# Queries loaded without zeros, and matrix products of ones ahead of the first loads

## The chip, the core and the metric

The kernel runs on one core of a Trainium2 chip. Five engines work side by side, each with its own queue of instructions: TensorE (PE; its weight loads are listed apart as PEld), VectorE (DVE), ScalarE (ACT), GpSimd (POOL) and SyncE (SP), which here issues every DMA. The metric is the device time of one execution in microseconds (us), the median of several runs; lower is better.

## The reference

Attention over 8 batches, 8 heads, 576 positions and 64 features per head, followed by a mixing block:

```python
scores = scale * np.matmul(q, k.transpose(0, 1, 3, 2))
mask_plain = (rel >= 0) & (rel < 32)                              # heads 0..3
mask_dil = (rel >= 0) & (rel < 128) & (rel % 4 == 0)              # heads 4..7
attn = softmax(np.where(masks, scores, -1e9))
x = np.matmul(attn, v)            # heads side by side: (8, 576, 512)
theta = x @ w_theta
y = w_tok_r @ (x * cos(theta)) + w_tok_i @ (x * sin(theta))
u = x + y
out = u + np.maximum(u @ w_ch, 0.0)
```

Each query sees 32 keys at most. Positions of the dilated heads are reordered on the host, so that their 32 keys lie side by side too.

## The kernel before

**Tiles of the attention.** Heads go in pairs (four pairs `pr` per batch `b`, 32 pairs in all). A pair has 18 blocks of 32 queries, and each block meets the 64 keys around it. `scores(b, pr)` (L441) makes one matmul per block (L468): the stationary operand is 128 x 64, 64 features of each of the two heads by 32 queries of each. It is block-diagonal: the half of a column that belongs to the other head is zero, so one matmul over 128 partitions serves both heads. The host array `qT` holds these zeros (L1006 to L1010), and so one pair's queries are 128 x 1152 words, of which half are zeros; they come with one DMA (L221, and L282 for batch 0). The keys come as 128 x 608 words (L223, L284). Matmuls of float32 appear twice in the trace, so the 18 blocks of a pair are 36 weight loads and 36 matmuls.

**Batch 0** goes ahead of all else. `first_loads` (L270) issues on SP, in this order: the masks, two identities, and queries and keys of the four pairs, then the values. The mask is added by matmuls of `mskb` with the identity `idb` (L424), and the score matmuls add onto it. DVE takes the row maximum and subtracts it (L430, L433), ACT exponentiates (L493), DVE sums (L495), POOL normalises (L510), PE transposes (L561, `flip`), and `pv` (L603) multiplies by the values (L617). ACT copies the result out of PSUM (L581, `x_evac`); for the pairs 2 and 3 that copy writes with a step of four words, since it undoes the reordering of positions. Then follow theta (L667), sines and cosines, the token mixing `y` (L850) and the channel mixing `c` (L882). Weights are unpacked on the way (`unpack`, L311; L332 is its first step on DVE).

**Order of the work.** Up to the middle of batch 1, the class `Order` sets the order: a planner that gives each task a rank and each step a cost, and starts on each engine the ready task with the lowest rank. Loads enter it by their words (`dma(2 * S)` for a pair's queries). What it lays out is pinned in that order on PE, DVE, ACT, POOL and SP. From then on `phase` (L889) writes the scores of the next batches, the mixing units and the values' products out in turn; PE keeps this order.

**Loads in flight.** A DMA signals one of eight semaphores, used in turn. A DMA therefore waits until the one issued eight before it has landed. In the steady part two buffers `q` (pool `attn`, L218) take turns, and the load of a pair waits for the scores two pairs back.

Of the kernel before, what the change touches and what calls it, by code (L numbers as in the profile page):

```python
# [8 lines left out]
F32 = mybir.dt.float32  # L9
# [28 lines left out]

FG0 = {4: ("zl2", "zl6"), 0: ("zl3", "zl7"), 1: ("zh3", "zh7")}
COS_PSUM, SIN_PSUM = True, True  # L40
KORD = (0, 4, 1, 5, 2, 6, 3, 7, 8)
TP0 = {4: "s", 0: "s", 1: "x", 2: "t", 3: "s"}
TP = {4: "t", 0: "s", 1: "s", 2: "t", 3: "s"}
# [108 lines left out]
def build(ctx, tc, qT, kT, vw, wth, wtk, wch, maskb, ident, identb, outT):  # L152
# [60 lines left out]
    def load_qk(n):  # L213
        if n >= B * NP:
            return
        b, pr = divmod(n, NP)
        r = yield from take("qk", 2)
        q = ap.tile([128, 2 * NJ, 2 * QB], F32, tag="q", name=f"q{b}_{pr}")  # L218
        k = ap.tile([128, S + 32], F32, tag="k", name=f"k{b}_{pr}")
        yield "DMA", dma(2 * S)  # L220
        pin(nc.sync.dma_start(q, qT[b, pr]))  # L221
        yield "DMA", dma(S + 32)
        pin(nc.sync.dma_start(k, kT[b, pr]))  # L223
        qks[b, pr] = (q, k, r)
        signal(("qk", b, pr))
# [12 lines left out]
    def load_vb(n):  # L238
# [12 lines left out]
        vs["b", b, pr] = (vb, r)  # L251
        signal(("vb", b, pr))

    KE = S + 32
    first_k = hp.tile([128, 10 * HS], F32R, tag="wt_b", name="first_k").bitcast(F32)
    first_v = hp.tile([128, 8 * HS], F32R, tag="wt_a", name="first_v").bitcast(F32)
# [13 lines left out]
    def first_loads():  # L270
# [3 lines left out]
        for pr in range(NP):  # L274
            yield from take(f"xh{pr}", 1, 0)
            yield from take(f"u{pr}", 1, 0)
            pqs.append(hp.tile([128, 2, S], F32R, tag=f"xh{pr}", name=f"P0_{pr}").bitcast(F32)[:, 0])
            q = hp.tile([128, 2, S], F32R, tag=f"u{pr}", name=f"q0_{pr}").bitcast(F32)
            q = q.rearrange("p a b -> p (a b)").rearrange("p (a b) -> p a b", b=2 * QB)
            k = first_k[:, KE * pr:KE * pr + KE]  # L280
            yield "DMA", dma(2 * S)
            pin(nc.sync.dma_start(q, qT[0, pr]))  # L282
            yield "DMA", dma(KE)
            pin(nc.sync.dma_start(k, kT[0, pr]))  # L284
            qks[0, pr] = (q, k, None)
            if pr == 0:
                yield "DMA", dma(128)
                pin(nc.sync.dma_start(idt, ident))
            signal(("qk", 0, pr))
# [11 lines left out]
    def consts():  # L301
        yield "DVE", 60
        pin(nc.vector.memset(halfpi, math.pi / 2))
        for n in range(2):
# [2 lines left out]
            pin(nc.gpsimd.memset(t, 0.0))  # L307
            pts.append(t)
        signal("pts")

    def unpack(src, sz, name, stage, early, n, key):  # L311

# [128 lines left out]
    def scores(b, pr):  # L441
# [3 lines left out]
        if pr >= 1:  # L445
            yield None, ("sc", b, pr - 1)
        q, k, rqk = qks[b, pr]
        if b == 0:
            P, rp = pqs[pr].rearrange("p (a b) -> p a b", b=BW), None
        else:  # L450
            rp = yield from take("P", 2)
            P = sp.tile([128, NJ, BW], F32, tag="P", name=f"P{b}_{pr}")
# [3 lines left out]
        for g0, g1 in ((0, 5), (5, NJ)):  # L456
# [8 lines left out]
            for n in range(g0, g1):  # L465
                for e in range(2):
                    qb = 2 * n + e
                    pe(nc.tensor.matmul(ps[64 * e:64 * e + 64, n - g0], q[:, qb],  # L468
                                        k[:, QB * qb:QB * qb + BW], start=not masked, stop=not masked or n == g1 - 1))
            if masked:  # L470
                go(row_max(b, ps, rel, P, mx, g0, g1, ("mask", b, pr, g0)))
# [481 lines left out]
    EA, LA, LA2 = ([(t, reserve(t)) for t in ts] for ts in (EARLY, LATE, LATE2))  # L953
    XH = {p: reserve(f"xh{p}") for p in range(NP)}
    UH = {d: reserve(f"u{d}") for d in range(NC)}
    od.live = True
    go(first_loads(), 0)
    go(consts(), 0)
# [36 lines left out]
def _arrays(inp):  # L995
# [7 lines left out]
        return a  # L1003

    q, k, v = perm(q), perm(k), perm(v)
    qT = np.zeros((B, NP, 2, D, 2 * NJ, 2, QB), q.dtype)  # L1006
    qh = q.reshape(B, NP, 2, 2 * NJ, QB, D).transpose(0, 1, 2, 5, 3, 4)
    for hh in range(2):
        qT[:, :, hh, :, :, hh] = qh[:, :, hh]
    qT = qT.reshape(B, NP, 128, 2 * NJ, 2 * QB)  # L1010
    kT = np.zeros((B, NP, 128, S + 32), k.dtype)
    kT[..., 32:] = k.transpose(0, 1, 3, 2).reshape(B, NP, 128, S)
    vp = np.zeros((B, H, S + 32, D), v.dtype)
# [45 lines left out]
```

## Time and profile before

| | |
|---|---|
| median of 3 runs | 577.83 us (577.48 to 578.81) |
| the profiled execution | 577.82 us |
| its span, first to last instruction | 576.0 us |
| PE, PEld busy | 550.5 us (96%), 501.6 us (87%) |
| DVE, ACT, POOL busy | 378.0, 345.2, 222.2 us |
| moved by DMA | 81.9 MB |

A row of the timeline gives start, duration, engine, line, operation, destination and sources, and how many instructions are merged into it; in brackets stands how long the engine had been idle before and what ended this. A row of the windows view gives the busy time of each engine in a stretch (with the number of instructions), then the TensorE clock that the throttle granted (1.00 is full), the mean busy share of the 16 DMA engines, and GB/s. In a row of the waits view stand the total, the number of waits and the longest. In the chain of waits each row is a start, a duration and what it was; "issue" is time without a recorded cause. DMA rows give the size of one and the median time from issue to landing.

### The profile page before, as it was taken

To read this page: it belongs to the slowest core of one execution; us is meant where nothing else is said; L and a number is where in the kernel's file an instruction comes from. 1 tells how busy PE (TensorE), PEld (TensorE's weight loads), DVE (VectorE), ACT (ScalarE), POOL (GpSimd) and SP (SyncE) were. 2 spreads that over 40 slices of the span, in tenths; PEclk is the share of its full clock that TensorE was granted. 3 is DMA by queue.
4 is the path that set the end of the run, shared out by engine and by line. 5 is a ranking of instruction groups with operands and counts; after the bars stand their busy time and mean duration, and the time that the engine had idled before them with its cause. 6 is when DMAs were issued, how large, how long until landed. Compare 5 with 4: busy or idle time off the path is not lost.

```text
span 576.0 us, 13996 instructions
## 1 busy us (share of the span) xinstructions
PE 550.5 (96%) x5464; PEld 501.6 (87%) x5464; DVE 378.0 (66%) x1156; ACT 345.2 (60%) x939; POOL 222.2 (39%) x206
## 2 busy tenths in 40 slices
PE   5997799999999999999999999999999999999997
PEld 4744688879999899988999899988999899989997
DVE  3879798865666668756776768756775767445112
ACT  1498967768555784369555785359556695266110
POOL 2228855525224352226324253226323353325220
PEclk9999699899999999999999999999999999999999
DMA  8991437601747046540746146550747123321002
GB/s 303 400 368 28 165 105 245 216 0 63 231 150 193 32 162 210 169 127 20 268 143 172 64 148 202 181 136 11 252 146 190 69 83 102 77 89 65 18 1 83
DMA packets 45586, 81.91 MB, mean 142 GB/s; under 512 B 3920, under 2 KB 19024, under 8 KB 45520
## 3 DMA queue, kind: packets, MB, share of 16 engines
q1 hardware_dynamic: 45520, 81.02, 43.7%
q8 instruction: 43, 0.70, 0.5%
q14 instruction: 23, 0.19, 0.1%
HBM read 64.49 MB, written 16.52 MB: 141 GB/s over the span
## 4 chain that ended last, share of the span: by engine, by line
DVE 34%; ACT 30%; PE 25%; issue 5%; POOL 2%; DMA 2%; SPq 0%; ACTq 0%; POOLq 0%; DVEq 0%
DVE pt L525 16%; PE y L850 11%; ACT P L504 11%; PE c L882 6%; PE th L685 3%; DVE P L409 3%; ACT K L698 3%; ACT K L787 3%; DVE xh L599 3%; ACT th L796 2%; ACT zh L644 2%; DVE xq L729 2%; DVE K L789 2%; ACT cos L705 2%; ACT x L581 2%
## 5 line engine op out<-in xcount | busy, mean ns | idle before, releaser
L830 POOL TENSOR_TENSOR u<-x,u 128x288 fp32r<-128x288 f32 x64 | 54.7, 858 | 184.6 <-ACT u L828 184.6
L525 DVE STREAM_TRANSPOSE pt<-P 32x288 f32<-32x288 f32 x224 | 105.1, 469 | 12.0 <-POOL P L510 8.9
L882 PE MATMUL c<-u,late_wc 128*128 128x288 f32 x768 | 110.2, 296 | 2.8 <-DVE x L859 2.8
L882 PEld LDWEIGHTS c<-u,late_wc 128*128 128x128 f32 x768 | 106.0, 188 | 6.8 <-DVE x L859 4.0
L850 PE MATMUL y<-wtkh,zh 128*128 128x288 f32 x288 | 90.3, 314 | 1.1 <-ACT zh L644 1.1
L850 PE MATMUL y<-wtkh,zl 128*128 128x288 f32 x288 | 86.2, 299 | 4.0 <-POOL zl L646 4.0
L646 POOL TENSOR_TENSOR zl<-g,zh 128x512 fp32r<-128x512 f32 x40 | 52.3, 1316 | 97.5 <-ACT zh L644 84.5
L504 ACT ACTIVATE P<-P,mx 128x64 f32<-128x64 f32 x216 | 72.0, 335 | 25.8 <-DVE mx L498 25.8
L850 PE MATMUL y<-wtkl,zh 128*128 128x288 f32 x288 | 85.9, 298 | 0.0
L828 ACT CAST u<-x 128x288 fp32r<-128x288 f32 x64 | 26.9, 429 | 86.2 <-DVE x L825 85.5
L685 PE MATMUL th<-wthh,xh 128*128 128x512 f32 x224 | 74.8, 395 | 0.3 <-DVE g L784 0.3
L850 PE MATMUL y<-late_wt_b,zh 128*128 128x288 f32 x320 | 68.1, 297 | 0.0
L825 DVE TENSOR_TENSOR x<-y,x 128x288 f32<-128x288 f32 x64 | 28.1, 448 | 53.6 <-PE y L850 53.5
L850 PEld LDWEIGHTS y<-wtkh,zl 128*128 128x128 f32 x288 | 55.1, 191 | 4.7 <-POOL zl L646 4.7
L850 PEld LDWEIGHTS y<-wtkh,zh 128*128 128x128 f32 x288 | 54.9, 191 | 4.7 <-ACT zh L644 2.3
L850 PE MATMUL y<-late_wt_a,zh 128*128 128x288 f32 x256 | 56.3, 301 | 0.0
L850 PEld LDWEIGHTS y<-wtkl,zh 128*128 128x128 f32 x288 | 55.1, 191 | 0.3 <-issue 0.3
L510 POOL TENSOR_TENSOR P<-P,sm 128x576 f32<-128x576 f32 x32 | 37.5, 1172 | 41.1 <-DVE sm L508 18.1
L850 PEld LDWEIGHTS y<-late_wt_b,zh 128*128 128x128 f32 x320 | 51.4, 189 | 0.3
L685 PEld LDWEIGHTS th<-wthh,xh 128*128 128x128 f32 x224 | 42.0, 188 | 9.2 <-DVE g L784 0.6
L850 PE MATMUL y<-late_wt_b,zl 128*128 128x288 f32 x160 | 47.4, 296 | 0.0
L581 ACT COPY x<-o 128x576 f32<-128x576 f32 x32 | 29.4, 919 | 28.4 <-PE o L617 19.1
(108 smaller groups left out, 1106.3 us busy)
## 6 DMA issues: line engine op xcount, KB each, us to landing
q<-in_qT_dram SPq DMA_DIRECT2D x32, 576.0 KB, 5.2
va<-in_vw_dram SPq DMA_DIRECT2D x30, 320.0 KB, 3.2
k<-in_kT_dram SPq DMA_DIRECT2D x28, 304.0 KB, 5.5
out_dram<-x SPq DMA_DIRECT2D x28, 288.0 KB, 2.4
vb<-in_vw_dram SPq DMA_DIRECT2D x29, 256.0 KB, 3.8
xd<-xq SPq DMA_DIRECT2D x24, 288.0 KB, 5.1
xn<-xd SPq DMA_DIRECT2D x24, 256.0 KB, 3.4
st_wtk<-in_wtk_dram SPq DMA_DIRECT2D x8, 576.0 KB, 8.8
```

The lines of the kernel that those rows point to most:

```text
L409: pin(nc.vector.tensor_tensor_reduce(out=P[:, n], in0=ps[:, n - g0], in1=mskb[:, mask_of(pr, n)], op0=ALU.add, op1=ALU.max, scale=1.0, sca ...
L504: table(nc.scalar.activation(P[:, n], P[:, n], AF.Exp, bias=mx[:, n:n + 1], scale=SCALE, accum_out=sm[:, n:n + 1]))
L510: pin(nc.gpsimd.tensor_tensor(P, P, sm.unsqueeze(2).to_broadcast([128, NJ, BW]), op=ALU.mult))
L525: pin(nc.vector.transpose(pmats[b, pr][k0:k0 + QB, :, hh, QB * e:QB * e + QB], P[p0:p0 + QB, :, QB * o:QB * o + QB]))
L581: pin(nc.scalar.copy(dst, src))
L646: pin(nc.gpsimd.tensor_tensor(lo, z, hi.bitcast(F32), op=ALU.subtract))
L685: pe(nc.tensor.matmul(pt, l, r, start=(n == 0), stop=(n == 3 * NC - 1)))
L825: pin(nc.vector.tensor_tensor(x[:, ts], ps, x[:, ts], op=ALU.add))
L828: pin(nc.scalar.copy(uh[b, d][:, ts], x[:, ts]))
L830: pin(nc.gpsimd.tensor_tensor(ul[b, d][:, ts], x[:, ts], uh[b, d][:, ts].bitcast(F32), op=ALU.subtract))
L850: pe(nc.tensor.matmul(ps, l[:, cs], r, start=(n == 0), stop=(n == 3 * NK - 1)))
L882: pe(nc.tensor.matmul(ps, l[:, cs], r[:, ts], start=(n == 0), stop=(n == 3 * NC - 1)))
```

## The change

Four things change.

- The host no longer writes the zeros. `qT` is 128 x 576 words per pair: 64 features of head one, then 64 of head two, and along a row the 18 blocks innermost (a query of position 32 n + r in its head lies at word 18 r + n).
- A pair's queries come with two DMAs of 64 x 576 words, each into its own half of the partitions and of the columns of a tile 128 x 2 x 576. The other halves are zeroed: in batch 0 by DVE, two memsets per pair; later two tiles `qbufs` take turns for the whole run and are zeroed once, by POOL.
- The stationary operand of a score matmul now is `q[:, :, qb]`: 64 columns with a step of 18 words (72 bytes), where it was 64 words side by side.
- DVE writes ones into a 128 x 512 bf16 tile ahead of all else, and PE multiplies it by itself 14 times into an unused PSUM tile ahead of its first mask matmul.

```diff
+WARM_UP = 14
...
-        q = ap.tile([128, 2 * NJ, 2 * QB], F32, tag="q", name=f"q{b}_{pr}")
+        q = qbufs[r % 2]
...
-        yield "DMA", dma(2 * S)
-        pin(nc.sync.dma_start(q, qT[b, pr]))
+        yield "DMA", dma(S)
+        for hh in range(2):
+            rs = slice(64 * hh, 64 * hh + 64)
+            pin(nc.sync.dma_start(q[rs, hh], qT[b, pr, rs]))
...
+    qbufs = [cp.tile([128, 2, S], F32, name=f"q{n}") for n in range(2)]
...
             q = hp.tile([128, 2, S], F32R, tag=f"u{pr}", name=f"q0_{pr}").bitcast(F32)
-            q = q.rearrange("p a b -> p (a b)").rearrange("p (a b) -> p a b", b=2 * QB)
+            for hh in range(2):
+                pin(nc.vector.memset(q[64 * hh:64 * hh + 64, 1 - hh], 0.0))
...
-            yield "DMA", dma(2 * S)
-            pin(nc.sync.dma_start(q, qT[0, pr]))
+            yield "DMA", dma(S)
+            for hh in range(2):
+                rs = slice(64 * hh, 64 * hh + 64)
+                pin(nc.sync.dma_start(q[rs, hh], qT[0, pr, rs]))
...
+        for q in qbufs:
+            for hh in range(2):
+                yield "POOL", 580
+                pin(nc.gpsimd.memset(q[64 * hh:64 * hh + 64, 1 - hh], 0.0))
...
+        q = q.rearrange("p h (r n) -> p (h r) n", n=2 * NJ)
...
-                    pe(nc.tensor.matmul(ps[64 * e:64 * e + 64, n - g0], q[:, qb],
+                    pe(nc.tensor.matmul(ps[64 * e:64 * e + 64, n - g0], q[:, :, qb],
...
+    ones = cp.tile([128, DM], BF16, name="ones")
+    nc.vector.memset(ones, 1.0)
+    busy = ps_v.tile([128, 2 * DM], F32, tag="v", name="busy")
+    for n in range(WARM_UP):
+        pe(nc.tensor.matmul(busy[:, :DM], ones[:, :128], ones, start=True, stop=True))
...
-    qT = np.zeros((B, NP, 2, D, 2 * NJ, 2, QB), q.dtype)
-    qh = q.reshape(B, NP, 2, 2 * NJ, QB, D).transpose(0, 1, 2, 5, 3, 4)
-    for hh in range(2):
-        qT[:, :, hh, :, :, hh] = qh[:, :, hh]
-    qT = qT.reshape(B, NP, 128, 2 * NJ, 2 * QB)
+    qT = q.reshape(B, H, 2 * NJ, QB, D).transpose(0, 1, 4, 3, 2).reshape(B, NP, 128, S)
```

The planner sees half the words for a query load and lays its part out anew. Three places matter.

SP at the start, before: the loads of batch 0 (`q_0` is pair 0's queries; all keys go into one tile `first_k`; DMAHWn is one of the eight semaphores of the loads).

```order
L282 DMA q_0_105<-in_qT_dram 128x1152
L284 DMA first_k<-in_kT_dram 128x608
L288 DMA idt<-in_ident_dram 128x128
L282 DMA q_1_115<-in_qT_dram 128x1152
L282 DMA q_2_122<-in_qT_dram 128x1152
L284 DMA first_k<-in_kT_dram 128x608 [waits DMAHW0_49]
L282 DMA q_3_155<-in_qT_dram 128x1152 [waits DMAHW1_49]
L284 DMA first_k<-in_kT_dram 128x608 [waits DMAHW2_49]
L293 DMA first_v<-in_vw_dram 128x1152 [waits DMAHW3_49]
```

SP at the start, now:

```order
L293 DMA q_0_123<-in_qT_dram 64x576 x2
L295 DMA first_k<-in_kT_dram 128x608
L299 DMA idt<-in_ident_dram 128x128
L293 DMA q_1_136<-in_qT_dram 64x576 x2
L295 DMA first_k<-in_kT_dram 128x608 [waits DMAHW0_49]
L293 DMA q_2_147<-in_qT_dram 64x576 [waits DMAHW1_49]
L293 DMA q_2_147<-in_qT_dram 64x576 [waits DMAHW2_49]
L295 DMA first_k<-in_kT_dram 128x608 [waits DMAHW3_49]
L293 DMA q_3_170<-in_qT_dram 64x576 [waits DMAHW4_49]
```

The order is the same, with two loads where there was one; so the wait for the load eight before comes after fewer pairs: with the keys of pair 1, where it was with those of pair 2.

PE at the start, before (`s_0_0` is the first half of pair 0's scores in PSUM):

```order
L424 LDWEIGHTS idb
L424 MATMUL s_0_0_118<-mskb,idb 128x64
L424 MATMUL s_0_0_118<-mskb,idb 128x256
L468 MATMUL s_0_0_118<-first_k,q_0_105 64x64 x10
L424 MATMUL s_0_5_135<-mskb,idb 128x256
```

PE at the start, now (the first two rows stand 14 times):

```order
L977 LDWEIGHTS ones
L977 MATMUL busy<-ones 128x512
L439 LDWEIGHTS idb [waits DMAHW1_49]
L439 MATMUL s_0_0_141<-mskb,idb 128x64 [waits DMAHW0_49]
L439 MATMUL s_0_0_141<-mskb,idb 128x256
L484 MATMUL s_0_0_141<-first_k,q_0_123 64x64 [waits DMAHW3_49,DMAHW4_49,DMAHW2_49,DVE_49]
L484 MATMUL s_0_0_141<-first_k,q_0_123 64x64 x9
```

The products of ones stand ahead of everything; the first score matmul waits for two query loads, the keys, and DVE's memsets.

SP around the loads of `w_ch` (`st_wch`, channel weights), before:

```order
L250 DMA vb_1_997<-in_vw_dram 128x512
L221 DMA q_1_1072<-in_qT_dram 128x1152
L325 DMA st_wch_1063<-in_wch_dram 128x1024
L325 DMA st_wch_1113<-in_wch_dram 128x1024
L223 DMA k_1_1073<-in_kT_dram 128x608
L234 DMA va_3_1110<-in_vw_dram 128x640
L250 DMA vb_2_1111<-in_vw_dram 128x512
```

The same place now:

```order
L253 DMA vb_1_1023<-in_vw_dram 128x512
L340 DMA st_wch_1067<-in_wch_dram 128x1024
L224 DMA q_91<-in_qT_dram 64x576 x2
L226 DMA k_1_1105<-in_kT_dram 128x608
L237 DMA va_3_1143<-in_vw_dram 128x640
L340 DMA st_wch_1146<-in_wch_dram 128x1024
L253 DMA vb_2_1144<-in_vw_dram 128x512
```

The first channel weights now go ahead of a query load, the second behind two more loads. Elsewhere the planner moves some matmuls of theta and of the first mixing units by a few places in batches 0 and 1; behind that, the rows of PE, DVE, ACT and POOL are the same as before.

## The prediction

> **What bounds the kernel now.** I read the busy time by stretches first (PE, PEld, DVE, ACT, POOL, then clock, DMA share, GB/s), since one share over the whole span hides the stages.
>
> ```profile
> 0.00:2.00 2.00, 0.00 (x0) 0.00 (x0) 0.06 (x1) 1.27 (x1) 1.47 (x6) 1.00 0.07 14
> 2.00:4.00 2.00, 0.45 (x2) 0.13 (x2) 0.00 (x0) 0.01 (x1) 0.78 (x1) 1.00 0.74 187
> 4.00:6.00 2.00, 0.00 (x0) 0.00 (x0) 0.00 (x0) 0.00 (x0) 0.00 (x0) 1.00 1.06 381
> 6.00:8.00 2.00, 0.97 (x18) 1.00 (x20) 0.00 (x0) 0.00 (x0) 0.00 (x0) 1.00 0.92 321
> 8.00:10.00 2.00, 2.00 (x27) 1.35 (x23) 1.19 (x3) 0.00 (x0) 0.00 (x0) 1.00 0.97 359
> ...
> 200.00:300.00 100.00, 98.91 (x1095) 93.44 (x1094) 71.42 (x259) 62.27 (x181) 37.06 (x34) 1.00 0.49 153
> ```
>
> From about 140 us on PE is busy 99 us of 100, DVE 71: TensorE is the bound, and DMA (share under 0.5) is not. The first 8 us are loads, with the DMA engines full from 4 us. In between DVE sets the pace, after a start in which it waits:
>
> ```profile
> 8.40:12.00 3.60, 2.19 (x5) 1.00 1.03 400
> 12.00:16.00 4.00, 3.14 (x10) 1.00 1.03 419
> 16.00:20.00 4.00, 3.01 (x10) 1.00 1.03 395
> 20.00:24.00 4.00, 3.45 (x9) 1.00 1.04 409
> ...
> 40.00:60.00 20.00, 18.83 (x43) 0.94 0.29 96
> ```
>
> ```profile
> DVE mx L430 <- PE s L468: 9.6, 4, 7.5
> ```
>
> These rows are DVE alone. It works 11.79 of the 15.6 us from 8.4 to 24, so 3.8 are idle; the waits from 8 us on say that the row maxima wait for the scores. The chain of waits has the cause:
>
> ```profile
> 3.53 6.60 DMA first_k<-in_kT_dram
> ...
> 11.65 0.49 DVE mx L430
> ...
> 13.70 1.27 PE s L468 x20
> ...
> 16.35 0.87 PE pT L561 x20
> ```
>
> Pair 1's scores wait for its keys (landed 10.13 us); then PE itself is the pace until 17 us. Its clock there has to be read from the matmuls:
>
> ```profile
> 10.27 1.34 PE L468 MATMUL s<-first_k,q 128*64 128x64 f32 x20
> ...
> 18.02 0.80 PE L468 MATMUL s<-first_k,q 128*64 128x64 f32 x20
> ...
> 143.01 1.27 PE L468 MATMUL s<-k,q 128*64 128x64 f32 x36
> ```
>
> The same 20 matmuls take 1.34 us at 10 us and 0.80 at 18: 27 ns more for each. The granted clock column says 1.00 in both stretches, so at the start it doesn't show the slow state.
>
> **The change part by part.** *Earlier loads.* Sizes from the list of DMA issues, with the median time to landing:
>
> ```profile
> q<-in_qT_dram SPq DMA_DIRECT2D x32, 576.0 KB, 5.2
> first_k<-in_kT_dram SPq DMA_DIRECT2D x4, 304.0 KB, 7.3
> xn<-xd SPq DMA_DIRECT2D x24, 256.0 KB, 3.4
> xn<-xd SPq DMA_DIRECT2D x6, 128.0 KB, 2.6
> mskb<-in_maskb_dram SPq DMA_DIRECT2D x1, 96.0 KB, 2.0
> idt<-in_ident_dram SPq DMA_DIRECT2D x1, 64.0 KB, 4.5
> idb<-in_identb_dram SPq DMA_DIRECT2D x1, 32.0 KB, 1.7
> ```
>
> Up to pair 1's keys that is 96 + 32 + 576 + 304 + 64 + 576 + 304 = 1952 KB, or 2.00 MB. By the windows 2 x (14 + 187 + 381 + 321 + 359) = 2524 KB had moved by 10 us, so some 0.52 MB of later loads shared the time. Halving two query loads takes 0.59 MB away: 1.41 + 0.52 = 1.93 MB, reached at 8.4 us (1.81 MB by 8, then 359 GB/s). These keys land 1.7 us earlier. Pair 0's scores (started 7.0) come 0.3 MB sooner, 0.8 us.
>
> ```profile
> 1.64 0.42 SPq L282 DMA_DIRECT2D q<-in_qT_dram  x1
> 2.11 0.43 SPq L284 DMA_DIRECT2D first_k<-in_kT_dram  x1
> ```
>
> An issue takes 0.47 us with its gap, so pair 1's keys, behind two more issues, go out 0.94 us later, at 4.5; with the 2.0 of the mask load as the shortest time to landing that is 6.5, still before 8.4. If a 64-partition load is no shorter than the whole one, the gain is nothing and 0.9 is lost: these are the ends. The 128 KB load (64 partitions) landed in 2.6 us and the 256 KB one in 3.4, nearer to a fixed part plus bytes; I take 1.7. Later the 32 more issues lie on SP, which waits for buffers there.
>
> *Faster scores at the start.* The one stretch of y matmuls back to back that regained the clock shows how long that takes:
>
> ```profile
> 67.69 0.31 PE L850 MATMUL y<-wtkh,zl 128*128 128x288 f32 x1
> 67.82 0.42 PE L850 MATMUL y<-wtkh,zh 128*128 128x288 f32 x1
> 68.04 0.44 PE L850 MATMUL y<-wtkl,zh 128*128 128x288 f32 x1
> ...
> 71.33 0.30 PE L850 MATMUL y<-wtkh,zh 128*128 128x288 f32 x1
> ```
>
> Slow, 288 columns take 0.24 us (68.04 to 68.28), and full speed is back after 3.4 us of them. 512 columns are then 0.43 us; 14 of them 6.0 us if all are slow, 3.3 at the 0.13 of 67.69 to 67.82. From about 1.3 us (DVE starts at 0.8 and first writes the ones) they end between 4.6 and 7.3, so they cover 3.4 us and end about where the scores can start (6.2): at the worst 1 us late. I expect the scores at full clock, 0.54 us less for 20 and 0.43 for 16.
>
> *Sum at the start.*
>
> ```profile
> 8.40 0.49 DVE L430 TENSOR_REDUCE mx<-s 128x5 f32<-128x320 f32 x1 [7.54 <-PE s L468]
> ...
> 12.05 0.74 DVE L495 TENSOR_REDUCE sm<-P 128x9 f32<-128x576 f32 x1
> ```
>
> DVE has for a pair a maximum and a subtraction over 320 columns (0.49 each) and over 256 (some 0.42 each), the sum (0.74) and two short operations: 2.9 us. Pair 0's scores can start at 6.2 and its first maximum, 1.1 us of masks and scores later, at 7.3 instead of 8.4. Pair 1's scores are there 0.8 after the keys, at 9.2, and DVE runs through: pair 2's maximum at 12.2 instead of 15.02, 2.8 us earlier. Of the idle time after it (0.99 us from 16 to 20 and 0.55 up to 24) I count a third. That makes 3.3 us; all idle gone and 1.1 from the earlier start would be 4.9, and if loads and clock both fail it is nothing. DVE is busy 94% from 40 to 60, so the shift is carried on.
>
> *Memsets.* DVE writes eight times 576 words; its sum above reads 576 in 0.74 us, so at most 5.9 us (below it any less), and with the ones done by about 7.2, while DVE is idle until 8.4 now. If they weren't covered, pair 0's first maximum would move by that. POOL's four have half the words of this row's two:
>
> ```profile
> 0.73 2.05 POOL L307 MEMSET pt<- 128x1152 f32 x2 [0.29 <-POOLq L1045]
> ...
> 13.67 1.15 POOL L510 TENSOR_TENSOR P<-P,sm 128x576 f32<-128x576 f32 x1 [10.89 <-DVE sm L508]
> ```
>
> 2.1 us, done at 5, and POOL is next needed at 13.67. No cost.
>
> *Less traffic later.* Once more a load ends a wait:
>
> ```profile
> 99.62 5.64 DMA st_wch<-in_wch_dram
> ```
>
> With 0.3 MB less in front (0.7 us at 400 GB/s), DVE may gain up to that twice; the changed order of the planner may take as much. I count 0.2, with -1 and +1.4 as ends.
>
> *Weight loads with a step.* From 140 us on, PE is the bound, and a score's weight load now reads words 72 bytes apart. PE has no such read here. The nearest row is ACT's copy out of PSUM, the same shape without and with a step of four words (16 bytes) in what it writes:
>
> ```profile
> 20.63 0.64 ACT L581 COPY x<-o 128x576 f32<-128x576 f32 x1
> ...
> 28.97 1.17 ACT L581 COPY x<-o 128x576 f32<-128x576 f32 x1
> ```
>
> Pair 0 takes 0.64, pair 2 (step 16 bytes) 1.17: nearly double. So the ends are no cost and a doubling. I take none for the forecast, since this row is a write by another engine, and because a matmul of a float32 pair loads its weights while the one before runs. This is the weakest point, and makes the rival below.
>
> The Trainium skill, "SBUF — State Buffer", section "Specifications (TRN2)", says that SBUF has lines of 16 bytes and that full bandwidth takes two hits per line. The two ACT rows agree; for PE no run here shows it yet. By that rule the result would be that of rival 1.
>
> *Total.* 3.3 + 0.2 = 3.5 us off the span of 576.0, so 572.5; with the 1.8 us outside it (577.82 in the profiled execution, median 577.83) **574.3 us**. Likeliest case's own range: 571.5 (4.9 + 1.4) to 577.
>
> **Rivals.**
>
> 1. *The stepped weight loads set PE's pace.* 36 matmuls take 1.27 us, of which 0.22 is the last one's own length: 30 ns each.
>
> ```profile
> 140.00:500.00 360.00, 27.14 (x792) 24.97 (x792) 1.00 0.46 141
> ```
>
> These 792 score matmuls (22 pairs) lie where PE is full; 30 ns more for each is 23.8 us, so 574.3 + 23.8 = 598 us; half of it 586. It decides from 3.5 / 792 = 4.4 ns per load. For it: the ACT rows, PE 99% busy. Against it: a read, not a write, and PE's loads partly lie under matmuls.
>
> 2. *Two half loads are no faster than the whole.* For it: 64 partitions only per load, one more issue, and an earlier wait for the load eight before. Pair 1's keys then land at 11.0, its maximum, with 0.54 us saved by the clock, comes at 12.0 (11.65 now), and pair 2's 2.9 later, at 14.9 (15.02 now). With the third of the later idle time that is 0.6 us: 577.2 us.
>
> The Trainium skill, same page, section "Can I just issue two DMAs to hit both halves?", says that 64 partitions reach half the ports and that two such loads gain only 6% by being in flight together. By it the query loads save next to nothing. The xn rows (128 KB in 2.6 us, 256 KB in 3.4) leave it open.
>
> 3. *The products of ones don't raise the clock, or it falls back* in the waits between scores. Then only the loads count, 1.7 us: 576.1 us.
>
> **How the numbers follow.** Forecast 0.50, rival 1 0.25, rival 2 0.14, rival 3 0.11. About 0.2% (1.2 us) is what can be told from no change here. The forecast and rival 3 are faster (0.61), rival 2 is the same (0.14), rival 1 slower (0.25). The range goes from 570.5 (the low end, with a little for waits I don't see) up into rival 1 until no more than 2 in 10 are left out, at its half price and a little more: 588.
>
> **What would show it.** Score matmuls before 17 us: 20 in 0.80 us, not 1.34. Pair 1's keys at about 8.4 us. DVE's idle time up to 24 us down by 2 to 3 us and pair 2's first maximum near 12. From 140 us on 36 score matmuls still in 1.2 to 1.3 us; 2 us and more would be rival 1. Wrong would be a stage after 140 us that is longer, or a start that is shorter while the end is not.

## The result, and the profile after

| | before | with the change |
|---|---|---|
| median (lowest to highest) | 577.75 us (576.67 to 579.83, 6 runs) | 600.86 us (599.22 to 602.71, 6 runs) |
| ratio, 95% interval | | 1.0397 (1.0369 to 1.0426) |
| the profiled execution, its span | 577.82, 576.0 | 599.95, 598.2 |
| moved by DMA | 81.9 MB | 72.5 MB |

The kernel became 4.0% slower. 23.1 us were added, where the forecast took 3.5 off, and the range (570.5 to 588) doesn't hold the time. Rival 1 had 598.

The page of the changed kernel: its first line, the busy time, the chain of waits by engine, and the groups of the score line (now L484; busy us, mean ns of one, idle time ahead).

```profile
span 598.2 us, 14069 instructions
PE 582.6 (97%) x5478; PEld 532.3 (89%) x5478; DVE 385.0 (64%) x1165; ACT 347.8 (58%) x939; POOL 225.4 (38%) x210
...
PE 84%; DMA 6%; DVE 4%; POOL 2%; ACT 1%; SPq 1%; issue 1%; DVEq 0%; POOLq 0%
...
L484 PE MATMUL s<-k,q 128*64 128x64 f32 x1008 | 65.3, 283 | 0.2 <-DVE K L805 0.2
L484 PEld LDWEIGHTS s<-k,q 128*64 128x64 f32 x1008 | 61.3, 210 | 4.2 <-issue 3.1
```

The same rows of the kernel before (the second from the list of groups with shapes kept apart):

```profile
DVE 34%; ACT 30%; PE 25%; issue 5%; POOL 2%; DMA 2%; SPq 0%; ACTq 0%; POOLq 0%; DVEq 0%
...
L468 PE MATMUL s<-k,q 128*64 128x64 f32 x1008 | 37.5, 229 | 0.0
```

PE is busy 32 us more than before, and its share of the chain went from 25 to 84%. The 1008 score matmuls from batch 1 on take 65.3 us of PE's time, where they took 37.5.

The windows view of the score line alone, before (L468) and after (L484): stretch, its length, PE, PEld, then clock, DMA share and GB/s.

```profile
140.00:520.00 380.00, 27.14 (x792) 24.97 (x792) 1.00 0.46 139
```

```profile
140.00:520.00 380.00, 49.96 (x792) 47.81 (x792) 1.00 0.40 118
```

The same 792 matmuls take 22.8 us more, 28.8 ns each, at the same full clock. The forecast's rival 1 had 30 ns each.

The timeline of the changed kernel, at the places that the forecast named.

```profile
1.46 5.14 PE L977 MATMUL busy<-ones 128*128 128x512 bf16 x14 [1.46 <-DVE ones L974]
...
6.68 1.37 PE L484 MATMUL s<-first_k,q 128*64 128x64 f32 x20
...
9.52 1.38 PE L484 MATMUL s<-first_k,q 128*64 128x64 f32 x20
...
14.22 0.49 DVE L445 TENSOR_REDUCE mx<-s 128x5 f32<-128x320 f32 x1 [0.67 <-PE s L484]
...
152.56 2.24 PE L484 MATMUL s<-k,q 128*64 128x64 f32 x36
```

36 score matmuls take 2.24 us where they took 1.27. The 20 ahead of 17 us take 1.37, though the ones ran for 5.14 us just ahead of them. Pair 1's scores start at 9.52 (10.27 before; 8.4 plus a little was expected), pair 2's first maximum at 14.22 (15.02 before; 12.2 expected).

The loads of the first microseconds, in the windows view of the changed kernel:

```profile
4.00:6.00 2.00, 2.00 (x7) 0.80 (x6) 1.49 (x4) 0.00 (x0) 1.09 (x2) 1.00 0.92 263
6.00:8.00 2.00, 2.00 (x26) 1.55 (x24) 0.78 (x2) 0.00 (x0) 0.00 (x0) 1.00 0.91 271
8.00:10.00 2.00, 2.00 (x29) 1.68 (x29) 1.56 (x4) 0.00 (x0) 0.00 (x0) 1.00 0.93 246
```

The DMA engines are nearly as full as before (share 0.91 to 0.93; 0.92 to 1.06 before), but move 246 to 271 GB/s where they moved 321 to 381. Half of the query bytes went, and a quarter of the rate with them (780 of 1061, the three stretches added).

**Where the 22.2 us of span lie.** The value product of batch 2's first pair is a good mark (from the timelines; before at 148.00, after at 151.46). From there to the end it was 428.0 us before and is 446.7 now: 18.7 us of the loss come behind the mark, 3.5 ahead of it.

### The profile page after: what moved, and what is told of

Same layout as the page of the kernel before. It is cut to its first block, busy times and chain, and to the rows that moved or that the text cites. A ratio compares the mean times of both kernels' runs of the same rounds, so it can differ in the third digit from the quotient of the medians.

```text
span 598.2 us, 14069 instructions
## 1 busy us (share of the span) xinstructions
PE 582.6 (97%) x5478; PEld 532.3 (89%) x5478; DVE 385.0 (64%) x1165; ACT 347.8 (58%) x939; POOL 225.4 (38%) x210
## 4 chain that ended last, share of the span: by engine, by line
PE 84%; DMA 6%; DVE 4%; POOL 2%; ACT 1%; SPq 1%; issue 1%; DVEq 0%; POOLq 0%
PE y L866 38%; PE c L898 16%; PE th L701 12%; PE s L484 9%; PE o L633 5%; DMA st_wtk<-in_wtk_dram 2%; DMA st_wth<-in_wth_dram 2%; POOL zl L662 1%; DVE pt L541 1%; PE th L706 1%; DMA vb<-in_vw_dram 1%; DMA first_k<-in_kT_dram 1%; PE th L705 1%; DMA st_wch<-in_wch_dram 1%; DMA k<-in_kT_dram 1%
## 5 line engine op out<-in xcount | busy, mean ns | idle before, releaser
L898 PE MATMUL c<-u,late_wc 128*128 128x288 f32 x768 | 108.9, 295 | 0.0
L484 PE MATMUL s<-k,q 128*64 128x64 f32 x1008 | 65.3, 283 | 0.2 <-DVE K L805 0.2
L484 PEld LDWEIGHTS s<-k,q 128*64 128x64 f32 x1008 | 61.3, 210 | 4.2 <-issue 3.1
L526 POOL TENSOR_TENSOR P<-P,sm 128x576 f32<-128x576 f32 x32 | 38.8, 1212 | 47.6 <-ACT xh L609 16.1
## 6 DMA issues: line engine op xcount, KB each, us to landing
st_wtk<-in_wtk_dram SPq DMA_DIRECT2D x8, 576.0 KB, 7.9
```

The costliest lines, as they stand in the source:

```text
L484: pe(nc.tensor.matmul(ps[64 * e:64 * e + 64, n - g0], q[:, :, qb], k[:, QB * qb:QB * qb + BW], start=not masked, stop=not masked or n == g ...
L526: pin(nc.gpsimd.tensor_tensor(P, P, sm.unsqueeze(2).to_broadcast([128, NJ, BW]), op=ALU.mult))
L898: pe(nc.tensor.matmul(ps, l[:, cs], r[:, ts], start=(n == 0), stop=(n == 3 * NC - 1)))
```

## The experiments

Each kernel ran beside the kernel before on its chip; ratios are to that. Names of tiles and lines are those of the kernel that ran.

### 1. The step of the weight loads alone, and its size

The kernel before, with the words of `qT` in another order, so that the 64 columns of a block lie STEP words apart: 18 (72 bytes, as in the change), 2, 3 and 6. The loads stay whole, with their zeros; no ones.

```diff
+        qs = q.rearrange("p a b -> p (a b)").rearrange("p (g c s) -> p g c s", c=2 * QB, s=STEP)
...
-                    pe(nc.tensor.matmul(ps[64 * e:64 * e + 64, n - g0], q[:, qb],
+                    pe(nc.tensor.matmul(ps[64 * e:64 * e + 64, n - g0], qs[:, qb // STEP, :, qb % STEP],
...
+    qT = qT.reshape(B, NP, 128, 2 * NJ // STEP, STEP, 2 * QB).transpose(0, 1, 2, 3, 5, 4)
```

> The kernel before with its whole query loads and their zeros, and no products of ones; only the order of the words in a pair's queries is another, so that the 64 columns of a score's weight load lie 18 words (72 bytes) apart, as in the change. Theory S (the step sets PE's pace): a weight load about 210 ns instead of 138, the 36 score matmuls of a pair 2.2 us instead of 1.25, the time some 599 us (+21 or more). Theory L (the loss comes from the split loads and the planner's order): 138 ns as before and 578 us.

> As the run with a step of 18 words, but two blocks share a stretch, so the columns of a weight load lie 2 words (8 bytes) apart. If lines of 16 bytes with two hits each are what counts, this costs nothing: 138 ns, 578 us. If any step that isn't 1 takes the slow way, it is as slow as 18 words: 210 ns, 599 us. If the cost grows with the lines that are touched (64 columns: 16 lines without a step, 32 here, 64 with 18), it lies between, near 585 us.

> As the runs with steps of 18 and 2 words, with a step of 3 words (12 bytes): the 64 columns of a weight load touch 48 lines of 16 bytes, and every third line twice. If each change of line costs, a weight load is near 190 ns (three quarters of the way from 138 to 210); if a line must be hit twice or the load goes the slow way as a whole, 210; if only steps from 16 bytes on are slow, 138. Times: 593, 599 or 578 us.

> A step of 6 words (24 bytes): every column in a line of its own, as with 18 words, but a quarter of the distance. If the line is what counts, 210 ns and 599 us as with 18 words; if the distance counts, less than 210 ns.

18 words: 599.07 us (597.82 to 599.63), ratio 1.0362 (1.0343 to 1.0381). 2 words: 577.83, ratio 0.9998 (0.9981 to 1.0014). 3 and 6 words, one execution each: 586.81 and 599.16. The score line (L470) in the windows view, for 2, 3, 6 and 18 words:

```profile
140.00:520.00 380.00, 27.79 (x792) 25.63 (x792) 1.00 0.46 139
```

```profile
140.00:520.00 380.00, 38.90 (x792) 36.74 (x792) 1.00 0.46 139
```

```profile
140.00:520.00 380.00, 49.39 (x792) 47.24 (x792) 1.00 0.42 134
```

```profile
140.00:520.00 380.00, 49.77 (x792) 47.60 (x792) 1.00 0.42 133
```

PEld's time over 792 is the time from one weight load to the next. (By its own record a load lasts longer, since loads overlap: 138 ns before, then 138, 175, 208 and 210.) Beside it, how many lines of 16 bytes its 64 words touch in a partition:

| step in bytes | 4 (before) | 8 | 12 | 24 | 72 |
|---|---|---|---|---|---|
| lines of 16 bytes | 16 | 32 | 48 | 64 | 64 |
| ns per load | 31.5 | 32.4 | 46.4 | 59.6 | 60.1 |

The time is flat up to 32 lines; with 48 and 64 lines it is 0.93 to 0.97 ns per line. Past one word per line, distance costs nothing: 24 and 72 bytes are the same. For 12 bytes none of the three expected results came (175 ns where 138, 190 or 210 was expected); the cost goes by the number of lines. So the step alone makes the kernel 21 us slower, nearly all of the 23.1. The intervals of the two ratios overlap, so where the 2 us between them come from stays open.

The Trainium skill, "SBUF — State Buffer", section "Specifications (TRN2)", has lines of 16 bytes and asks for two hits per line for full bandwidth. The five sizes agree: two words per line (8 bytes) cost nothing, one word per line costs double.

### 2. The change without the step

Queries without zeros in two half loads, the memsets and the ones as in the change, but each half is put down as 18 runs of 32 words, so that a block's 64 columns lie side by side.

```diff
-            pin(nc.sync.dma_start(q[rs, hh], qT[b, pr, rs]))
+            pin(nc.sync.dma_start(q[rs, :, hh], qT[b, pr, rs].rearrange("p (n r) -> p n r", r=QB)))
```

> The change with its compact array, two loads per pair, zeros written once and products of ones, but the loads put the words where they lay before: 18 runs of 32 words, so a weight load reads 64 words side by side. Theory S: weight loads 138 ns again, at least 20 us faster than the changed kernel, 575 to 579 us. Theory L: still near 598 us. If runs of 128 bytes load slowly, the first keys land later than 8 us and the first 40 us are longer than before by 1 to 3 us.

580.96 us, ratio 1.0049 (1.0033 to 1.0066). Its windows at the start:

```profile
0.00:10.00 10.00, 6.96 (x55) 3.33 (x55) 6.59 (x14) 1.50 (x2) 4.49 (x10) 1.00 0.73 154
10.00:20.00 10.00, 8.85 (x165) 7.75 (x166) 5.74 (x16) 1.94 (x4) 1.36 (x2) 0.66 1.07 256
```

The score matmuls are as before (792 of them from 140 to 520 us: 27.14 us of PE), and the kernel is 19.9 us faster than the change, though slower than the 575 to 579 expected. With runs of 128 bytes the full DMA engines (1.07) move 256 GB/s from 10 to 20 us; in the change, with half loads of long runs, it is 357 GB/s, and before it was 395 to 419. So the step is gone, but the loads come late (PE waits 1.30 us for pair 1's keys, up to 10.63), and the clock falls back to 0.66.

### 3. Half of the bytes, in one load or in two

The kernel before, with only the first 9 of a pair's 18 blocks of queries loaded, in one DMA of 128 partitions or in two of 64; the other 9 blocks are computed from zeros. The bytes of queries are those of the change; no step, no ones.

```diff
-        pin(nc.sync.dma_start(q, qT[b, pr]))
+        pin(nc.sync.dma_start(q[:, :NJ], qT[b, pr, :, :NJ]))
...  or
+        for hh in range(2):
+            rs = slice(64 * hh, 64 * hh + 64)
+            pin(nc.sync.dma_start(q[rs, :NJ], qT[b, pr, rs, :NJ]))
```

> The kernel before, where each query load brings only its first 576 words per partition in one DMA over 128 partitions, and the second half of the tile is zeroed once (by DVE for batch 0, by POOL for the two later tiles); so the scores of the later nine blocks are computed from zeros, in the same number of matmuls. It has the change's bytes and memsets, without its split, its step and its products of ones. If bytes at full rate are worth what the forecast said: pair 1's keys at 8.4 us instead of 10.1, the values' product of pair 3 (31.7 us before) 2 to 4 us earlier, the time 574 to 576 us. If something else sets the pace: 577.5 to 579.

> As the run before it, with the same bytes in two DMAs of 64 partitions each, as the change has them. If 64-partition loads use half of the way into memory: 250 GB/s instead of 380 between 4 and 10 us at a DMA share over 0.9, pair 1's keys 1 us or more later than with whole loads, and the time 1 to 3 us longer than with whole loads. If the split is harmless, both runs are alike within 0.2%.

One load: 576.49 us (574.74 to 577.62, 10 runs; 574 to 576 expected), ratio 0.9979 (0.9963 to 0.9994). Two loads: 580.47 (578.22 to 581.31, 10 runs), ratio 1.0038 (1.0019 to 1.0057). Windows and timeline of the first (scores at L473) and of the second (L477):

```profile
6.00:8.00 2.00, 2.00 (x35) 1.66 (x33) 0.92 (x2) 0.00 (x0) 0.00 (x0) 1.00 1.00 325
8.00:10.00 2.00, 2.00 (x32) 1.45 (x28) 1.02 (x4) 0.64 (x1) 0.00 (x0) 1.00 0.97 351
```

```profile
8.70 1.15 PE L473 MATMUL s<-first_k,q 128*64 128x64 f32 x20
```

```profile
6.00:8.00 2.00, 1.66 (x23) 1.35 (x24) 0.28 (x1) 0.00 (x0) 0.00 (x0) 1.00 0.85 235
8.00:10.00 2.00, 1.44 (x19) 1.00 (x18) 1.56 (x4) 0.00 (x0) 0.00 (x0) 1.00 1.06 252
```

```profile
10.11 1.33 PE L477 MATMUL s<-first_k,q 128*64 128x64 f32 x20 [0.67 <-DMA first_k<-in_kT_dram]
```

The same bytes: in whole loads pair 1's scores start at 8.70 us, as the forecast had it; in half loads at 10.11 (10.27 before). At a DMA share near 1 the half loads run at 235 to 252 GB/s. Pair 0's scores start at 5.67 with whole loads and at 6.34 with half ones (7.03 before), so a part of the gain was there at first. In the total the split takes back all that the zeros gave, and more: 4 us between the two medians. Half loads also take longer to issue, and pair 1's keys go out at 5.13 us instead of 3.53. The lower rate and the later issues were not separated; with the DMA engines busy at 0.85 to 1.06 from 6 to 10 us, the rate is the likelier cause.

The Trainium skill, "SBUF — State Buffer", section "Can I just issue two DMAs to hit both halves?", says that two such loads together gain only 6% over one. The two kernels agree in kind: two half loads in flight moved fewer bytes per us than one whole load (235 to 252 GB/s against 325 to 351). One half load by itself was not run.

### 4. The ones alone, and the same time in short ones

The kernel before with the 14 products of ones. In the second run they are 96 products of 64 columns, about as long in all, but 192 PE instructions (each has its weight load) instead of 28.

```diff
+    ones = cp.tile([128, DM], BF16, name="ones")
+    nc.vector.memset(ones, 1.0)
+    busy = ps_v.tile([128, 2 * DM], F32, tag="v", name="busy")
+    for n in range(WARM_UP):
+        pe(nc.tensor.matmul(busy[:, :DM], ones[:, :128], ones, start=True, stop=True))
...  or
+        pe(nc.tensor.matmul(busy[:, :64], ones[:, :128], ones[:, :64], start=True, stop=True))
```

> The kernel before with the 14 products of ones alone. Expected if the clock at the start is worth something: pair 0's 20 first matmuls 0.80 us instead of 1.34, pair 2's first maximum 14.0 us instead of 15.0, the time 576.3 us. If the stages after 24 us take the gain back (loads or the order of DVE and ACT): the same first 20 us, but 577.5 to 578.

14 products: 580.24 us (578.48 to 580.47), ratio 1.0039 (1.0018 to 1.006), 0.4% slower; 576.3 or at most 578 was expected. Its timeline, PE and one row of DVE:

```profile
7.06 0.80 PE L469 MATMUL s<-first_k,q 128*64 128x64 f32 x20
9.98 0.80 PE L469 MATMUL s<-first_k,q 128*64 128x64 f32 x20 [0.68 <-DMA first_k<-in_kT_dram]
...
18.56 0.62 PE L618 MATMUL o<-pt,first_v 128*64 128x64 f32 x14 [1.14 <-issue]
...
24.69 0.68 PE L562 MATMUL pT<-idt,P 64*64 64x64 f32 x14 [0.88 <-issue]
...
25.40 0.42 DVE L537 COPY pt<-pT 64x256 f32<-64x256 f32 x1 [1.18 <-PE pT L562]
...
103.06 0.43 PE L425 MATMUL s<-mskb,idb 128*128 128x64 bf16 x2 [3.38 <-ACT P L486]
```

The ones do what they are for: 20 score matmuls in 0.80 us from the first pair on, and the first product of the values starts at 16.55 instead of 18.65. Then PE stands still twice, in the middle of a row of like matmuls, for 1.14 and 0.88 us, and nothing in the profile ends these waits ("issue"). The second holds DVE for 1.18 us, so that its second step on the theta weights starts at 25.74 us (25.66 before), and by the product of pair 3 (31.75; 31.66 before) nothing is left of the 2.1 us. Near 100 us PE then waits 3.38 us for ScalarE (1.95 before), and the clock from 100 to 120 us is 0.83 (0.91 before); batch 2 starts 2.4 us late. Why ScalarE is later there was not found.

What are the two waits? The page lists two DMA queues named "instruction"; the larger has 43 packets and 0.70 MB, 16 KB each. From the trace's DMA records, the first two of these packets at the start, and PE's wait without a cause, in us:

| kernel | 1st packet | PE goes on | 2nd packet | PE goes on |
|---|---|---|---|---|
| 14 ones | 16.03 to 17.13 | 18.56 | 22.09 to 23.07 | 24.69 |
| two matmuls per block, batch 0 (section 6) | 13.09 to 14.09 | 15.38 | 19.31 to 20.38 | 21.71 |
| the same, batches 0 and 1 | 12.16 to 13.16 | 14.46 | 18.29 to 19.37 | 20.79 |
| the change | 15.83 to 16.80 | no wait | 21.85 to 22.87 | 24.37 |
| the change without ones | 16.73 to 17.83 | no wait | 22.81 to 23.83 | 25.25 |

PE goes on 1.3 to 1.6 us after a packet landed, and in all five the second wait ends with the same number of weight loads and matmuls behind it, 695 to 697. That reads as PE waiting for its own instructions. The run with 96 short products moves every place of the program 164 instructions further on in the stream:

> The kernel before with 96 products of ones of 64 columns ahead of the masks, where the run with ones alone had 14 of 512: about as long on PE, but 192 PE instructions (weight loads and matmuls) instead of 28, so that any place of the program is 164 instructions further on in PE's stream. Theory A (PE's idle times without a recorded cause, 1.14 us at 18.56 and 0.88 at 24.69 in that run, are PE waiting for its own instructions, which come in pieces of about 250, each asked for when PE has come to a certain count and not sooner than some 6.1 us after the last): the pieces are asked for earlier, so both idle times are gone or under 0.3 us, the first pieces start at about 7 to 9 us instead of 16.0, the values' product of pair 2 starts at 23.7 to 24.7 instead of 25.29, and the total is 0.5 to 2 us below that run's 580.24, unless the stage near 100 us takes it back. Rival B (the idle times belong to these places of the program, or to the full DMA engines at these times): they are still there within 0.3 us of their size, the product of pair 2 at 25.2 or later.

577.71 us (576.22 to 579.82, 10 runs), ratio 0.9996 (0.9981 to 1.0011).

```profile
10.03 0.80 PE L469 MATMUL s<-first_k,q 128*64 128x64 f32 x20 [1.08 <-DMA first_k<-in_kT_dram]
...
13.01 1.34 PE L469 MATMUL s<-first_k,q 128*64 128x64 f32 x20
...
28.41 0.39 PE L618 MATMUL o<-pt,vb 128*64 128x64 f32 x5 [1.04 <-issue]
```

Both waits are gone from their places, and the first packet starts at 9.35 us (7 to 9 was expected). A wait of 1.04 us stands at a new place, 1.45 us after the third packet landed (25.86 to 26.96), with 950 weight loads and matmuls done: 253 after the 697. So theory A holds for the mechanism. Its number for pair 2 (23.7 to 24.7) missed: 26.23, since here the mean clock from 10 to 20 us fell to 0.66, and the scores of 13.01 take 1.34 us again. The windows view shows the clock:

```profile
10.00:20.00 10.00, 9.07 (x166) 7.97 (x167) 6.09 (x17) 1.55 (x4) 1.80 (x2) 0.66 1.03 409
```

The run therefore tells what the waits are, not what the kernel would gain without them. It is 2.5 us below the run with 14 products, but its wait for ScalarE near 100 us is also shorter (2.09 us), and how much of that comes from the instructions stays open.

### 5. The change without the ones

> The change without its ones and their 14 products; all else as in the change. Theory A (the step costs 21 us, the rest of the +23 is the ones and the split loads): 598.5 to 600, at or below the change by 0.5 to 2 us. Rival B (the ones help in the whole change as forecast, since the scores run at full clock): 601.5 to 603, above the change. First scores in both: 20 matmuls 1.3 us instead of the 1.37 that the change shows if they are bound by the step, 1.6 or more if step and low clock add up.

599.6 us (598.66 to 599.71), ratio 1.0367 (1.0343 to 1.0391). The change itself has 1.0397 (1.0369 to 1.0426): the intervals overlap, so at most the ones cost a little. The first scores without the ones, and the third pair's once the clock is up:

```profile
6.32 1.42 PE L484 MATMUL s<-first_k,q 128*64 128x64 f32 x20 [2.78 <-DMA first_k<-in_kT_dram]
...
13.22 1.37 PE L484 MATMUL s<-first_k,q 128*64 128x64 f32 x20
```

Under the step, 20 matmuls take 1.42 us at the low clock and 1.37 at full clock. What the ones save on 20 dense matmuls (0.54 us) is 0.05 here: the weight load sets the pace either way.

### 6. The zeros left out without step and without split

Two ways to keep one whole load of 128 x 576 words. First: batch 0, or batches 0 and 1, with two matmuls per block, one per head, over 64 partitions; no zeros at all.

```diff
+                        for hh in range(2):
+                            rs, os = slice(64 * hh, 64 * hh + 64), 64 * e + QB * hh
+                            pe(nc.tensor.matmul(ps[os:os + QB, n - g0], q[rs, QB * qb:QB * qb + QB],
+                                                k[rs, QB * qb:QB * qb + BW], start=not masked,
+                                                stop=not masked or n == g1 - 1, tile_position=(64 * hh, os)))
```

> Batch 0 only: a pair's queries come as 128 x 576 words without zeros in ONE load, and each block's scores are two matmuls, one per head, over 64 partitions and 32 columns; nothing is zeroed, no step in the weights, no ones; batches 1 to 7 as before. Theory A (what costs the start of the change is the split of the load over partitions): pair 0's scores at about 5.7 us, pair 1's at 8.4 to 8.8 as in the run with half of each load left out, the values' product of pair 0 at 15.6 to 16.5 us; total 575 to 577. Rival B (36 small matmuls per pair where there were 18 make PE the pace at the start, at the low clock): pair 0's scores take 2 us and more instead of 1.15 to 1.34, the product of pair 0 at 17.5 or later, total 578 or more.

> The same for batches 0 and 1, whose loads lie where the DMA engines are full (up to about 100 us). Theory A: the loads of batch 1 free another 4 x 0.29 MB, 2.9 us at 400 GB/s, of which DVE gains a third as in the start, so up to 1 us below the run with batch 0 alone: 574.5 to 576.5. Rival B (start gains are lost again at the idle stretch of PE near 100 us, after which the clock is low): the values' product of batch 2 stays at 148 us, total 577 to 578.5.

582.78 us, ratio 1.0087 (1.0066 to 1.0108), and 582.19, ratio 1.0079 (1.0059 to 1.01). The timeline of the second (scores at L477, transposes at L574):

```profile
5.66 1.29 PE L477 MATMUL s<-first_k,q 64*32 64x64 f32 x40 [2.15 <-DMA first_k<-in_kT_dram]
...
8.60 1.29 PE L477 MATMUL s<-first_k,q 64*32 64x64 f32 x40
...
14.46 0.35 PE L477 MATMUL s<-first_k,q 64*32 64x64 f32 x9 [1.08 <-issue]
...
20.79 0.80 PE L574 MATMUL pT<-idt,P 64*64 64x64 f32 x20 [2.50 <-issue]
```

The totals lie in rival B's range, but neither theory had the reason. The loads are early (5.66 and 8.60), and 40 small matmuls are no slower than 20 large ones (1.29 us; 1.34 before). But the stream is longer by 144 weight loads and 144 matmuls per batch, and PE waits 1.08 and 2.50 us for it. The product of pair 2 starts at 29.69 (25.89 before).

Second: batch 0 with the same load into a free tile, and two copies per pair that write it into the block-diagonal tile (0.67 us on ScalarE, 0.46 on VectorE or 0.67 on GpSimd); PE's instructions as before.

```diff
+        a = q[rs, :, QB * hh:QB * hh + QB], raw[rs].rearrange("p (n j) -> p n j", j=QB)
+        if hh == 0:
+            pin(nc.scalar.copy(*a))
+        elif pr == 0:
+            pin(nc.vector.tensor_copy(*a))
+        else:
+            pin(nc.gpsimd.tensor_copy(*a))
```

> Batch 0 only: a pair's queries come without zeros in ONE load of 128 x 576 words, and are then written into the block-diagonal tile of before by two copies of 64 x 576 words (ScalarE for head one; VectorE for head two of pair 0, GpSimd for the others), the zeros by eight memsets on VectorE; matmuls, their number and the dense weight loads as before, no ones. Theory A (the gain of the run with half of each load left out, 576.5, can be had if neither step, nor split load, nor more PE instructions are paid for it): pair 0's scores at 6.0 to 6.6 us (a copy of about 0.7 us behind the load, 7.0 before), pair 1's at about 8.7 to 9.2 (10.27), the values' product of pair 0 at 16 to 17 (18.65), total 576 to 577.3. Rival B (the copies come too late, or the gain is lost again where PE idles near 100 us): the values' product of pair 0 at 17.5 or later, or of batch 2 at 148 us or later; total 577.5 to 579.

580.41 us (579.79 to 584.69, 9 runs), ratio 1.0057 (1.0033 to 1.0081). Its timeline on PE:

```profile
6.02 1.33 PE L493 MATMUL s<-first_k,q 128*64 128x64 f32 x20 [2.39 <-DMA first_k<-in_kT_dram]
...
16.77 1.22 PE L642 MATMUL o<-pt,first_v 128*64 128x64 f32 x36
...
24.50 2.18 PE L692 MATMUL th<-st_wth,x 128*64 128x512 f32 x4 [1.10 <-DVE st_wth L353]
26.61 0.80 PE L642 MATMUL o<-pt,va 128*64 128x64 f32 x20
...
49.63 0.66 PE L784 MATMUL xn<-idt,x 128*128 128x128 f32 x4 [2.40 <-DVE K L814]
56.38 0.63 PE L784 MATMUL xn<-idt,x 128*128 128x128 f32 x4 [2.59 <-DVE K L775]
```

The start is nearly as theory A has it: scores at 6.02 and 9.41 (8.7 to 9.2 expected), the first product at 16.77, 1.9 us early. Then the planner, which counts half the words for the loads and the copies besides, has put four theta matmuls ahead of the product of pair 2 (26.61; 25.89 before), and between 45 and 60 us PE waits 2.40 and 2.59 us for VectorE (before, three waits there came to 3.88 us). Batch 2 starts at 149.98, later than before as in rival B, and the total lies above both ranges. What each of these places costs was not tested. No version here computes the whole result and beats the kernel before.

**All of them side by side**, from the timelines of the profiled executions, in us:

| kernel | values' product, pair 0 | pair 3 | batch 2, pair 0 | span | from there to the end |
|---|---|---|---|---|---|
| before | 18.65 | 31.66 | 148.00 | 576.0 | 428.0 |
| 14 ones | 16.55 | 31.75 | 150.39 | 578.7 | 428.3 |
| 96 short ones | 19.36 | 33.12 | 148.37 | 576.4 | 428.0 |
| half of the bytes, one load | 15.64 | 32.65 | 144.87 | 573.0 | 428.1 |
| half of the bytes, two loads | 18.90 | 34.39 | 148.98 | 577.1 | 428.1 |
| two matmuls per block, batch 0 | 17.94 | 37.91 | 154.14 | 582.0 | 427.9 |
| the same, batches 0 and 1 | 17.03 | 36.46 | 152.04 | 580.1 | 428.1 |
| copies, batch 0 | 16.77 | 33.27 | 149.98 | 578.6 | 428.6 |
| the step alone | 19.13 | 32.07 | 152.10 | 597.8 | 445.7 |
| the change without ones | 18.61 | 34.30 | 152.00 | 597.9 | 445.9 |
| the change | 18.20 | 33.90 | 151.46 | 598.2 | 446.7 |

Two things stand out. From batch 2 on, all kernels with dense weights take 428 us (the steps of 2 words and section 2's kernel, not listed, 428.3 and 428.0), and those with the step of 18 words 446 to 447. And ahead of it the first column does not foretell the third: of the four kernels that start 1.6 to 3.0 us early, three reach batch 2 between 2.0 and 4.0 us late, and one 3.1 early (its profiled execution took 574.77 us, 1.7 under its median; that of the two half loads 578.90, 1.6 under its own).

## Why the prediction was wrong, step by step

**Weight loads with a step: "I take none".** This step failed, and with it the sign. The load of 64 columns takes 60 ns instead of 31. The two ends stood in the prediction (no cost, a doubling), and the doubling was right: rival 1's 30 ns against 28.6 to 28.8. What was wrong was the choice between the ends. The only row with a step of 16 bytes in the trace was the ScalarE copy, 0.64 against 1.17 us, and it was set aside because it was a write by another engine; the argument against it, that PE's loads partly lie under matmuls, had no row behind it. The rule of the Trainium skill that the prediction named beside that row ("SBUF — State Buffer", section "Specifications (TRN2)") is the one that the five sizes then bore out; row and rule together should have made rival 1 the likeliest case.

Rival 1's total, 598, came near 600.86 by a somewhat other sum than its own. Of the 792 matmuls, 756 lie behind the mark of batch 2. From there to the end the score line takes 21.8 us more of PE's time (47.66 against 25.87), and 18.7 us reach the end (17.7 with the step alone): PE is idle for 4.2 us there instead of 6.1, and its other matmuls take 1.2 us less. The group of the channel mixing shows both, before and after:

```profile
L882 PE MATMUL c<-u,late_wc 128*128 128x288 f32 x768 | 110.2, 296 | 2.8 <-DVE x L859 2.8
```

```profile
L898 PE MATMUL c<-u,late_wc 128*128 128x288 f32 x768 | 108.9, 295 | 0.0
```

Ahead of the mark lie 396 score matmuls, of which rival 1 counted 36. They take 7.0 us more of PE's time with the step alone, and the mark comes 4.1 us later (152.10 against 148.00). And the gain of 3.5 that rival 1 kept was not there.

**Earlier loads: "I take 1.7".** The bytes were counted rightly: with whole loads pair 1's scores start 1.6 us earlier (8.70 against 10.27). The choice that a half load is "nearer to a fixed part plus bytes" failed. It rested on the two xn loads, which are issued from 183 us on, where the DMA share is 0.46; at the start the engines are full, and the rate was 235 to 271 GB/s instead of 321 to 381. The issues were underrated too: in the change pair 1's keys go out at 5.15 us, where the prediction had 4.5. (The 2.0 us that it took for the shortest landing isn't the shortest of its list, which has 1.7; nothing hung on it.) Pair 0's part came out: without the ones its scores start at 6.32 (6.2 forecast). Rival 2 had this mechanism, but the two half loads cost more than it said: 580.47 against its 577.2.

**Faster scores at the start.** The ones end at 6.60 us (4.6 to 7.3 expected), after 5.14 us (3.3 to 6.0), and the clock is up: 0.80 us for 20 dense matmuls in the run with ones alone. In the change it buys 0.05 us instead of 0.54, since the stepped loads set the pace there; and the ones end 0.3 us after the scores could have started (6.32 without them). Rival 3 is refuted for the first pairs; that the clock can fall back after waits of PE is seen in two runs (0.66 from 10 to 20 us, sections 2 and 4).

**Sum at the start: 3.3 us, "so the shift is carried on".** Pair 2's first maximum came 0.8 us earlier instead of 2.8. The weight loads are in this too: PE has no gap from 1.46 to 12.2 us, and the scores of the pairs 0 and 1 take 2.06 us longer in it than dense ones at full clock (1.37 and 1.15 us in a pair, against 0.80 and 0.69 in section 4). The second half of the sum, that the shift is carried on, failed independently: even where the start was 1.6 to 3.0 us earlier, the shift was not carried on. That DVE is 94% busy from 40 to 60 us says that it sets the pace there, not that it may start earlier. PE's instructions come in pieces of about 250, some 6.1 us apart at the start (22.09 after 16.03, 18.29 after 12.16), and cap PE's progress up to 25 us; then come weights, and a planner's order that is another one in each kernel that loads other sizes.

**Memsets: no cost.** Right. The timeline of the changed kernel has DVE's first, POOL's four and pair 0's first maximum:

```profile
1.47 0.54 DVE L288 MEMSET q<- 64x576 f32 x1
...
2.73 2.40 POOL L324 MEMSET q<- 64x576 f32 x4
...
8.10 0.49 DVE L445 TENSOR_REDUCE mx<-s 128x5 f32<-128x320 f32 x1 [1.16 <-PE s L484]
```

DVE's eight take 0.54 us each, 4.3 in all, and DVE then idles until 8.10, waiting for PE.

**Less traffic later: 0.2 us.** Not to be told apart from the planner's new order: at the mark of batch 2 the kernels with other loads lie from 3.1 us early to 6.1 us late.

**The chances.** Slower had 0.25. The range ended at 588, inside rival 1 at a half price that never came: the cost is there in full from one word per 16-byte line on, and about half the price per load needs a step of 12 bytes (14.9 ns of 28.6; 586.81 us in one execution).

## What to carry to other kernels

Before a layout is changed to save bytes, look at what reads it: on a PE that is 99% busy, less traffic at a DMA share of 0.46 was worth nothing (the kernels that load half of the query bytes take 428.1 us from batch 2 on, 428.0 before), and 29 ns per weight load cost 21 us. Keep at least two columns of a float32 stationary operand in each 16-byte line (a step of 8 bytes was free, 12 cost half, 24 and 72 all of it), and keep loads on all 128 partitions while the DMA engines are full. A gain at the start is worth only what still stands at the next mark: here batch 2's first value product, from which every dense kernel takes 428 us.

## What the runs showed of the hardware that was not expected

- PE's weight load of 64 float32 columns on 128 partitions: 31 to 32 ns from one to another with 16 or 32 lines of 16 bytes touched, 46 with 48, 60 with 64. The distance beyond a line doesn't matter.
- PE can run dry of instructions in the first 30 us. Its stream comes in 16 KB packets over the same DMA engines as the data, about 250 weight loads and matmuls in each (about 445, then 695 to 697 and 950 at the ends), and PE goes on 1.3 to 1.6 us after a packet landed. The profile shows this as an idle time with "issue" in the middle of a row of like matmuls. In the two kernels that spared load bytes but added PE instructions there (section 6), the two waits came to 3.0 and 3.6 us, more than the early start of 0.7 and 1.6 us.
- The granted clock reads 1.00 at the start while the 20 matmuls take 1.34 us; 5 us of products of ones bring them to 0.80 from the first pair on. With waits of 0.68 and 0.81 us behind that the clock stayed up (14 products); with 1.08 and 0.81 (96 short ones) or 1.30 and 0.48 (section 2) the third pair's 20 matmuls took 1.34 and 1.33 us again.
